# Loading the expert layers' weights in six later pieces, in a fused mLSTM and mixture-of-depths kernel

## The chip, the cores and the metric

The kernel runs on one core of one Trainium2 chip. The metric is the time on the device, in microseconds (us), of one launch; the median of three runs before the change is 186.09 us (185.08 to 186.35). A core has TensorE (PE in the profile, and PEld for its weight loads), VectorE (DVE), ScalarE (ACT), GpSimd (POOL), and SyncE (SP), which here only issues transfers (DMA).

## The reference: what is computed

The first half is an mLSTM cell over 4 batches, 8 heads, 768 positions and heads of 40 numbers; the second half sends the 128 best-scoring positions of each batch through two layers.

```python
# mLSTM, for every position t of (B=4, H=8, S=768, D=40)
m_new  = np.maximum(f_gate[:, :, t] + m, i_gate[:, :, t])
f_stab = np.exp(f_gate[:, :, t] + m - m_new)
i_stab = np.exp(i_gate[:, :, t] - m_new)
C = f_stab[..., None, None] * C + i_stab[..., None, None] * np.einsum('bhd,bhe->bhde', vt, kt)
n = f_stab[..., None] * n + i_stab[..., None] * kt
y[:, :, t] = sigmoid(o_gate) * (C @ qt) / np.maximum(np.abs(n @ qt), 1.0)
# bridge: y (B,H,S,D) -> x (B, S, 320)
# mixture of depths, for every batch b
scores  = x[b] @ w_gate
top_idx = the 128 positions with the highest scores
h  = np.maximum(x[b, top_idx] @ w1, 0.0)          # w1: 320 x 1024
ye = h @ w2                                       # w2: 1024 x 320
out[b] = x[b];  out[b, top_idx] += sigmoid(scores[top_idx])[:, None] * ye
```

## The kernel before

The positions are cut into chunks of 128, six to a batch, so there are 24 steps `n`, with batch `b = n // 6` and chunk `c = n % 6`. A prologue does steps 0 and 1; steps 2 to 23 run in a loop. Inputs are loaded ahead: step `n` issues the loads of step `n + 4` (`AHEAD = 4`, five buffers), and all of them, the stores of the results and the weights, go through the one queue of SyncE, in program order.

```python
def load_qk(n):                       # two transfers, 160 KB each
    for j, src in enumerate((k, q)):
        load_heads(n, qk_t[n % NB][:, j, :, 0:D], src)
...
def load_w1(j):                       # w1: 320 rows as three blocks of 128, 128 and 64
    d0, w = HW[j]
    for p in range(0, 128, w):        # the block of 64 rows is loaded twice, into both halves
        nc.sync.dma_start(out=w1[p:p + w, j, :], in_=moe_w1[d0:d0 + w, :])

def load_w2(j):
    f = slice(j * NFC // 2, (j + 1) * NFC // 2)
    nc.sync.dma_start(out=w2[:, f], in_=moe_w2.rearrange("(f p) d -> p f d", p=128)[:, f])
```

One step, cut to what is spoken of below. `within` writes pH (line 427), `exchange` pIC (396, 402), `products` pS (370), `turned` transposes k and q of step n + 2 into T (313, copied by ScalarE in 314), `weights` makes W = exp(...) (346, 347), masked by GpSimd (352), and `weighted` multiplies P = pS * W on VectorE (376).

```python
def step(n):
    load(n + AHEAD)
    pH = within(P[n], v1)
    ...
    give = exchange(*steps[n + 1], loaded[n + 1][0], T[n + 1], wv[n + 1])
    pS[n + 1] = products(T[n + 1])
    ...
    num, sor = norm(nums.get(n), pH, so)
    nums[n + 1] = exchanged(*steps[n + 1], *give)
    P[n + 1] = weighted(pS[n + 1], W[n + 1])
    ...
    W[n + 2] = weights(*steps[n + 2])
    layer(b, c)                       # a part of the layers of an earlier batch
    turned(n + 2)
    ...
    result(b, c, num, sor)            # x, and its store: out_dram<-x, line 448
    score(b, c, state[b][0])
    compare(...)                      # ge, line 470
```

`layer` spreads the two layers of one batch over six steps: with c = 3, 4 and 5 it computes columns 0 to 2, 3 to 5 and 6 to 7 of the first layer, with c = 0, 1 and 2 of the next batch the same groups of the second. The first use of the weights is therefore in steps 9, 10, 11 (w1) and 12, 13, 14 (w2).

```python
def first(self, f0, f1):              # ph, line 545
    for f in range(f0, f1):
        for j in range(NDC):
            nc.tensor.matmul(self.ph[:, f % 4, :], w1[:, j, f * 128:(f + 1) * 128], self.xeT[:, j, :], ...)
...
def second(self, f0, f1):             # py, line 569
    if f0 == 0:
        self.py = ps_m.tile([K_, DM], FP, name="py", tag="m")
    for f in range(f0, f1):
        nc.tensor.matmul(self.py, self.hT[:, f, :], w2[:, f, :], start=(f == 0), stop=(f == NFC - 1))
```

After step 3 the loop makes the constants with which positions are ranked; after steps 3 to 7 it loads the weights.

```python
for n in range(3, N):
    step(n)
    if n == 3:
        nc.gpsimd.iota(iota_i, pattern=[[1, K_]], channel_multiplier=0)
        nc.vector.tensor_copy(out=iota_f, in_=iota_i)            # line 847
        nc.gpsimd.iota(token_i, pattern=[[L, NT]], channel_multiplier=1)
        nc.vector.tensor_copy(out=token, in_=token_i)            # line 852
        nc.vector.tensor_scalar(out=later, in0=token_i, ...)     # line 854
        nc.gpsimd.memset(ones_b, 1.0)
        ...
    if 3 <= n < 3 + NDC:
        load_w1(n - 3)
    elif 3 + NDC <= n < 5 + NDC:
        load_w2(n - 3 - NDC)
```

The last batch's layers stand alone in the tail. Its first layer keeps all eight columns in eight PSUM banks at once; two banks are those of pS, the others are drawn from pools. The pool `ps_m` has two buffers, used in turn, and py is drawn from it afterwards.

```python
def first_at_once(self, banks):
    ph = [p[:, 0, 0:K_] for p in pS_t] + [pool.tile([128, K_], FP, name="ph", tag=tag) for pool, tag in banks]
    for f, p in enumerate(ph):
        for j in range(NDC - 1):
            nc.tensor.matmul(p, w1[:, j, f * 128:(f + 1) * 128], self.xeT[:, j, :], start=(j == 0), stop=False)
    for f, p in enumerate(ph):
        nc.tensor.matmul(p, w1[e, NDC - 1, ...], self.xeT[e, NDC - 1], start=False, stop=True)
    for f, p in enumerate(ph):        # odd columns on VectorE (line 561), even ones on ScalarE (line 563)
        ...
...
last.first_at_once([(ps_t, "t"), (ps_t, "t"), (ps_h, "h"), (ps_c, "c"), (ps_m, "m"), (ps_m, "m")])
last.gate()
last.gated()
last.second(0, NFC)
last.leave()
```

Of the kernel before, what the change touches and what calls it, by code (L numbers as in the profile page):

```python
# [8 lines left out]
FP = mybir.dt.float32  # L9
BF = mybir.dt.bfloat16  # L10
HF = mybir.dt.float16
I32 = mybir.dt.int32
U32 = mybir.dt.uint32
AF = mybir.ActivationFunctionType
OP = mybir.AluOpType
# [6 lines left out]
def kernel(  # L22
# [20 lines left out]
    nc = tc.nc  # L43

    B, H, S, D = q.shape
    L = 128
    NT = S // L
# [6 lines left out]
    NFC = F_ // 128  # L54
    HW = [(c, min(128, DM - c)) for c in range(0, DM, 128)]
    NDC = len(HW)
    K_ = capacity
# [9 lines left out]
    const = ctx.enter_context(tc.tile_pool(name="const", bufs=1))  # L67
# [5 lines left out]
    ps_t = ctx.enter_context(tc.tile_pool(name="ps_t", bufs=2, space=PSUM))  # L73
    ps_s = ctx.enter_context(tc.tile_pool(name="ps_s", bufs=1, space=PSUM))
    ps_c = ctx.enter_context(tc.tile_pool(name="ps_c", bufs=1, space=PSUM))
    ps_h = ctx.enter_context(tc.tile_pool(name="ps_h", bufs=1, space=PSUM))
    ps_m = ctx.enter_context(tc.tile_pool(name="ps_m", bufs=2, space=PSUM))
# [6 lines left out]
    def load_gates(eng, dst, src, g):  # L84
        for c in range(3):
# [20 lines left out]
                            channel_multiplier=-1)  # L106
# [52 lines left out]
    for j in range(2):  # L159
        nc.vector.tensor_reduce(out=of[:, j:j + 1], op=OP.add, axis=AX.XY,  # L160
                                in_=ident.rearrange("p (g x) -> p g x", x=32)[:, :, 12 * j:12 * j + 12])
# [16 lines left out]
    m = gate.tile([BH, NT + 1], FP, name="m")  # L178
# [5 lines left out]
    pS_t = [ps_s.tile([128, NP, L], FP, name=f"pS{j}") for j in range(2)]  # L184
# [34 lines left out]
    def level(g, pm):  # L219

        own = gate.tile([NR, 3], FP, name="own", bufs=2)
        nc.vector.tensor_tensor_reduce(out=own, in0=pm, in1=third, scale=1.0, scalar=0.0, op0=OP.mult, op1=OP.add,
                                       accum_out=m_in[g])
        nc.vector.tensor_scalar(out=FM[g][:, 1], in0=FM[g][:, 1], scalar1=m_in[g], scalar2=None, op0=OP.max)
        nc.vector.tensor_scalar(out=nM[g], in0=FM[g][:, 1, L - 1:L], scalar1=-1.0, scalar2=None, op0=OP.mult)

    def split(g, j, eng, rows=slice(0, NR)):
        x, xs = (FM[g][rows, 1], a[g][rows])[j], [part[rows] for part in parts[j][g]]
        rest = gate.tile([NR, L], FP, name=f"rest{j}", bufs=2)[rows]
        eng.tensor_copy(out=xs[0], in_=x)  # L230
        eng.tensor_tensor(out=rest, in0=x, in1=xs[0], op=OP.subtract)
        eng.tensor_copy(out=xs[1], in_=rest)
        eng.tensor_tensor(out=xs[2], in0=rest, in1=xs[1], op=OP.subtract)
# [58 lines left out]
    w1 = const.tile([128, NDC, F_], FP, name="w1")  # L292
# [3 lines left out]

        return out[0:b + 1].rearrange("b s d -> (b s) d")

    def load_w1(j):

        d0, w = HW[j]
        for p in range(0, 128, w):
            nc.sync.dma_start(out=w1[p:p + w, j, :], in_=moe_w1[d0:d0 + w, :])

    def load_w2(j):
        f = slice(j * NFC // 2, (j + 1) * NFC // 2)
        nc.sync.dma_start(out=w2[:, f], in_=moe_w2.rearrange("(f p) d -> p f d", p=128)[:, f])

    def turn(qk, j, T, copy=nc.scalar.copy):
# [11 lines left out]
    def gated(n):  # L321

        so = loaded[n][2]
        nc.scalar.activation(out=so, in_=so, func=AF.Tanh, scale=0.5)
        nc.scalar.add(so, so, 1.0)
# [29 lines left out]
    def scaled_v(b, c, v1):  # L355
        if c == NT - 1:
            return None
        wv = work.tile([128, H, D1], FP, name="wv")
        nc.gpsimd.tensor_tensor(out=wv, in0=v1[:, :, 0:D1], op=OP.mult,  # L359
                                in1=cols[c][:, 0, b * H:(b + 1) * H].unsqueeze(2).to_broadcast([128, H, D1]))  # L360
        return wv
# [11 lines left out]
    def weighted(pS, W):  # L373
        P = work.tile([128, NP, 2, L], FP, name="P", bufs=2)
        for j in range(2):
            nc.vector.tensor_tensor(out=P[:, :, j, :], in0=pS[j], op=OP.mult,  # L376
                                    in1=W.rearrange("p (n a) t -> p n a t", a=2)[:, :, j, :])
        return P
# [119 lines left out]
    def number(sel, token):  # L498

        pidx = ps_m.tile([K_, 1], FP, name="pidx", tag="m")  # L500
        for t in range(NT):
            nc.tensor.matmul(pidx, sel[:, t, :], token[:, t:t + 1], start=(t == 0), stop=(t == NT - 1))
        return pidx

    def gather(b, pidx):
        idx = mod.tile([K_, 1], U32, name="idx")
        nc.vector.tensor_scalar(out=idx, in0=pidx, scalar1=float(b * S), scalar2=None, op0=OP.add)
        xe = xe_t[b % 2]
        nc.gpsimd.indirect_dma_start(out=xe[0:K_, 0:DM], out_offset=None, in_=rows(b),
                                     in_offset=bass.IndirectOffsetOnAxis(ap=idx, axis=0),  # L510
                                     bounds_check=(b + 1) * S - 1, oob_is_err=False)
        return idx, xe

    class Layers:
# [34 lines left out]

        def first_at_once(self, banks):  # L550

            ph = [p[:, 0, 0:K_] for p in pS_t] + [pool.tile([128, K_], FP, name="ph", tag=tag) for pool, tag in banks]
            for f, p in enumerate(ph):
                for j in range(NDC - 1):
                    nc.tensor.matmul(p, w1[:, j, f * 128:(f + 1) * 128], self.xeT[:, j, :], start=(j == 0), stop=False)
            for f, p in enumerate(ph):
                e = HALVES[f % 2]
                nc.tensor.matmul(p, w1[e, NDC - 1, f * 128:(f + 1) * 128], self.xeT[e, NDC - 1], start=False, stop=True)
            for f, p in enumerate(ph):
                if f % 2:  # L560
                    nc.vector.tensor_scalar(out=self.hT[:, f, :], in0=p, scalar1=0.0, scalar2=None, op0=OP.max)
                else:
                    nc.scalar.activation(out=self.hT[:, f, :], in_=p, func=AF.Relu)  # L563
# [39 lines left out]
    def stated(n):  # L603
        wv[n] = scaled_v(*steps[n], loaded[n][1])
# [185 lines left out]
    turned(2)  # L790
    P[1] = weighted(pS[1], W[1])
    stated(1)
    level(1, pm)
    split(1, 0, nc.gpsimd)
    moving()
# [8 lines left out]
    scales(1)  # L804
    gated(1)
    nc.vector.tensor_scalar(out=of_which, in0=which, scalar1=of[:, 1:2], scalar2=None, op0=OP.mult)
    P[2] = weighted(pS[2], W[2])

    load(1 + AHEAD)
# [3 lines left out]
    for j in range(2):  # L813
# [15 lines left out]
                            pattern=[[-1, L]], channel_multiplier=1)  # L829
# [11 lines left out]
    for n in range(3, N):  # L841
        step(n)
        if n == 3:
            iota_i = const.tile([128, K_], I32, name="iota_i")
            nc.gpsimd.iota(iota_i, pattern=[[1, K_]], channel_multiplier=0)
            iota_f = const.tile([128, K_], FP, name="iota_f")
            nc.vector.tensor_copy(out=iota_f, in_=iota_i)

            token_i = const.tile([128, NT], I32, name="token_i")
            nc.gpsimd.iota(token_i, pattern=[[L, NT]], channel_multiplier=1)  # L850
            token = const.tile([128, NT], HF, name="token")
            nc.vector.tensor_copy(out=token, in_=token_i)
            later = const.tile([128, NT], FP, name="later")
            nc.vector.tensor_scalar(out=later, in0=token_i, scalar1=-1.0, scalar2=float(S - 1), op0=OP.mult, op1=OP.add)
            ones_b = const.tile([128, 1], BF, name="ones_b")
            nc.gpsimd.memset(ones_b, 1.0)
            xe_t = [const.tile([128, NDC * 128], FP, name=f"xe{n}") for n in range(2)]
            for xe in xe_t:
                nc.gpsimd.memset(xe[:, DM:], 0.0)
        if 3 <= n < 3 + NDC:  # L860
            load_w1(n - 3)
        elif 3 + NDC <= n < 5 + NDC:
            load_w2(n - 3 - NDC)


    b, u = steps[-1]
# [2 lines left out]
    n = u * L  # L869
# [12 lines left out]
                                   op0=OP.is_ge, op1=OP.mult, accum_out=cnt[:, u:u + 1])  # L882
    pend = ps_h.tile([128, NT], FP, name="pend", tag="h")
    for t in range(NT):
# [3 lines left out]
                                   op0=OP.add, op1=OP.add)  # L888
# [3 lines left out]
    last = Layers(b, None, None)  # L892
# [6 lines left out]
    for j, (d0, w) in enumerate(HW):  # L899
# [3 lines left out]
        if j < 2:  # L903
# [4 lines left out]
    nc.scalar.copy(out=last.xeT[HALVES[1], 2], in_=pX[3][HALVES[1]])  # L908
    nc.vector.tensor_copy(out=last.xeT[HALVES[0], 2], in_=pX[2][HALVES[0]])
    last.idx, last.xe = gather(b, number(sel_h, token))  # L910
    last.first_at_once([(ps_t, "t"), (ps_t, "t"), (ps_h, "h"), (ps_c, "c"), (ps_m, "m"),
                        (ps_m, "m")])
    last.gate()
    last.gated()
    last.second(0, NFC)
# [27 lines left out]
```

## Time and profile before

| | |
|---|---|
| time, median of 3 (range) | 186.09 us (185.08 to 186.35) |
| span of the profiled execution, mean granted TensorE clock | 183.5 us, 0.986 |
| busy: PE, PEld | 170.4 us (93%), 141.5 us (77%) |
| busy: DVE, ACT, POOL | 135.9 us (74%), 102.3 us (56%), 106.4 us (58%) |
| transfers | 105,938 packets, 24.70 MB, mean 135 GB/s |
| share of the transfers' engines taken by SyncE's queue | 78.7% |
| chain that ended last | PE 64%, issue 10%, DVE 8%, DMA 7%, ACT 4% |
| one input's load: KB, issue to landing | 160.0 KB, 4.6 to 5.1 us (medians by input) |
| the weights' transfers, KB | w1: 2 x 512.0 and 2 x 256.0; w2: 2 x 640.0 |

The profile is one execution. Its page cuts the span into 40 equal slices of 4.6 us and gives a digit, in tenths, for each engine's busy share, the granted clock of TensorE and the transfers. A busy TensorE is not a TensorE at its peak: matmuls are pipelined, and their ends are modelled. The chain that ended last is followed back from the last instruction, at each step to what released it. In a timeline a line has its start, its busy time, the engine, the line of the kernel, the operation, what is written and read, and a count; a bracket gives the idle time before it and what ended that. SPq is SyncE's queue of issues; the time beside an issue is that of issuing it, not of moving the data.

### The profile page before, as it was taken

The page shows a single profiled execution, that of the slowest core. Times are in us where ns is not written, and L with a number is a line of the kernel's source. Part 1 is how long each engine was busy: PE and PEld are TensorE (multiplying, and loading weights), DVE is VectorE, ACT ScalarE, POOL GpSimd, SP SyncE. Part 2 cuts the span into 40 slices and gives each one's busy share as a digit, 9 for nine tenths or more (in the row PEclk, how much of TensorE's full clock was granted, in tenths as well). Part 3 has the DMA queues.
Part 4 walks back from the last instruction along what each step waited for, and adds up shares of the span by engine and source line. Part 5 has one row for each costly group of instructions (what it writes and reads, how often), then busy time and mean ns, then how long its engine had stood idle before and what let it go on. Part 6 is the DMA issues. An engine that isn't in the chain of part 4 may idle for free.

```text
span 183.5 us, 7319 instructions
## 1 busy us (share of the span) xinstructions
PE 170.4 (93%) x2992; PEld 141.5 (77%) x2992; DVE 135.9 (74%) x403; ACT 102.3 (56%) x250; POOL 106.4 (58%) x176
## 2 busy tenths in 40 slices
PE   7889997998999699999999999999999999989990
PEld 2578886787787587898797888898878979869860
DVE  7857788898789837568998969788988788584210
ACT  3285779899998687375545465465635652201100
POOL 7987986778887865137859633546666361113202
PEclk9999999999999969999999999999999999999998
DMA  3999998999998999999899999979972101010100
GB/s 73 148 149 136 159 163 156 156 173 231 156 205 178 151 266 147 222 157 183 160 177 165 192 170 190 163 145 178 176 80 75 39 36 41 36 39 36 38 4 36
DMA packets 105938, 24.70 MB, mean 135 GB/s; under 512 B 100656, under 2 KB 105264, under 8 KB 105904
## 3 DMA queue, kind: packets, MB, share of 16 engines
q1 hardware_dynamic: 105088, 22.77, 78.7%
q0 software_dynamic: 384, 1.31, 2.4%
q8 instruction: 24, 0.39, 1.0%
q10 hardware_dynamic: 432, 0.15, 0.6%
q14 instruction: 10, 0.08, 0.2%
HBM read 19.63 MB, written 4.59 MB: 132 GB/s over the span
## 4 chain that ended last, share of the span: by engine, by line
PE 64%; issue 10%; DVE 8%; DMA 7%; ACT 4%; SPq 2%; POOL 2%; POOLq 1%; DVEq 0%
PE pH L427 12%; PE pS L370 11%; PE pt L313 10%; PE ph L545 10%; PE py L569 5%; PE pIC L396 5%; PE pIC L402 4%; PE pW L346 3%; DMA qk<-in_q_dram 3%; DMA out_dram<-ye,idx 2%; DMA xe<-out_dram,idx 2%; PE pO L247 1%; DVE P L376 1%; DVE ge L470 1%; ACT T L314 1%
## 5 line engine op out<-in xcount | busy, mean ns | idle before, releaser
L347 ACT ACTIVATE W<-pW 128x512 f32<-128x512 f32 x48 | 26.1, 598 | 22.1 <-PE pW L346 21.9
L442 POOL TENSOR_TENSOR sor<-so,rec 128x320 f32<-128x320 f32 x24 | 17.8, 741 | 32.4 <-DVE rec L440 32.1
L376 DVE TENSOR_TENSOR P<-pS,W 128x512 f32<-128x512 f32 x48 | 30.9, 686 | 4.6 <-POOL W L352 2.4
L314 ACT COPY T<-pt 128x512 f32<-128x512 f32 x47 | 25.4, 589 | 14.1 <-PE pt L313 14.0
L352 POOL TENSOR_SCALAR_AFFINE_SELECT W<-W 128x512 f32<-128x512 f32 x46 | 30.6, 688 | 3.6 <-ACT W L347 3.6
L427 PEld LDWEIGHTS pH<-v,P 128*64 128x64 f32 x768 | 25.2, 141 | 8.8 <-DVE x L447 3.2
L427 PE MATMUL pH<-v,P 128*64 128x64 f32 x768 | 28.5, 229 | 2.7 <-issue 1.3
L313 PE MATMUL pt<-ident,qk 128*128 128x128 f32 x192 | 25.8, 276 | 1.8 <-DMA qk<-in_k_dram 1.0
L470 DVE SCALAR_TENSOR_TENSOR ge<-sb,sc,earlier 128x128 bf16<-128x128 f32 (+5 forms) x23 | 17.4, 761 | 13.0 <-ACT sb L464 13.0
L370 PE MATMUL pS<-T 64*64 64x64 f32 (+1 forms) x768 | 26.2, 255 | 0.0
L313 PEld LDWEIGHTS pt<-ident,qk 128*128 128x128 f32 x192 | 21.1, 141 | 4.1 <-ACT scr L455 1.4
L370 PEld LDWEIGHTS pS<-T 64*64 64x64 f32 x768 | 20.4, 132 | 1.9 <-issue 0.7
L569 PE MATMUL py<-w,hT 128*128 128x320 f32 x64 | 19.4, 444 | 0.4 <-ACT hT L563 0.4
L359 POOL TENSOR_TENSOR wv<-v,cols 128x328 f32<-128x328 f32 x20 | 14.9, 743 | 7.2 <-DMA v<-in_v_dram 5.2
L545 PE MATMUL ph<-xeT,w 128*128 128x128 f32 x144 | 18.1, 280 | 0.0
L545 PEld LDWEIGHTS ph<-xeT,w 128*128 128x128 f32 x144 | 16.7, 192 | 1.5 <-issue 1.5
L575 POOL DMA_INDIRECT out_dram<-ye,idx x4 | 4.6, 1140 | 19.6 <-DVE ye L573 19.6
L569 PEld LDWEIGHTS py<-w,hT 128*128 128x128 f32 x64 | 11.5, 191 | 5.6 <-issue 1.4
L396 PE MATMUL pIC<-C,T 128*64 128x82 f32 x320 | 15.8, 241 | 0.0
L396 PEld LDWEIGHTS pIC<-C,T 128*64 128x64 f32 x320 | 13.2, 141 | 0.3 <-issue 0.2
L384 POOL TENSOR_TENSOR C<-C,cols 128x328 f32<-128x328 f32 x16 | 13.1, 819 | 0.1
L432 DVE TENSOR_TENSOR pH<-num,pH 128x328 f32<-128x328 f32 x20 | 10.0, 499 | 3.7 <-PE pH L427 3.6
(166 smaller groups left out, 284.1 us busy)
## 6 DMA issues: line engine op xcount, KB each, us to landing
qk<-in_k_dram SPq DMA_DIRECT2D x24, 160.0 KB, 4.7
qk<-in_q_dram SPq DMA_DIRECT2D x24, 160.0 KB, 4.7
v<-in_v_dram SPq DMA_DIRECT2D x24, 160.0 KB, 5.1
so<-in_o_gate_dram SPq DMA_DIRECT2D x24, 160.0 KB, 4.6
out_dram<-x SPq DMA_DIRECT2D x24, 160.0 KB, 4.0
w<-in_moe_w_dram SPq DMA_DIRECT2D x2, 640.0 KB, 4.7
w<-in_moe_w_dram SPq DMA_DIRECT2D x2, 512.0 KB, 4.5
w<-in_moe_w_dram SPq DMA_DIRECT2D x2, 256.0 KB, 4.5
```

What stands on the lines that cost most here:

```text
L313: nc.tensor.transpose(pt[:, p, :], qk[:, j, 2 * p:2 * p + 2, :].rearrange("s a d -> s (a d)"), ident)
L314: copy(out=T[:, j], in_=pt)
L347: nc.scalar.activation(out=W[:, h0:h0 + 4, :], in_=pW, func=AF.Exp)
L352: nc.gpsimd.affine_select(out=W[:, h0:h0 + 4, :], in_=W[:, h0:h0 + 4, :], compare_op=OP.is_ge, fill=0.0, base=0, pattern=[[0, 4], [1, L]], ...
L370: nc.tensor.matmul(pS_t[j][s, p, ts], T[e, 0, p, s], T[e, 1, p, ts], start=True, stop=True)
L376: nc.vector.tensor_tensor(out=P[:, :, j, :], in0=pS[j], op=OP.mult, in1=W.rearrange("p (n a) t -> p n a t", a=2)[:, :, j, :])
L396: nc.tensor.matmul(pI[t, 2 * p * D1:2 * (p + 1) * D1], T[:, 1, p, t], C[:, p].rearrange("e a d -> e (a d)"), start=True, stop=True)
L427: nc.tensor.matmul(pH[t, 2 * p + j, :], P[:, p, j, t], v1[:, 2 * p + j, :], start=True, stop=True)
L442: nc.gpsimd.tensor_tensor(out=sor, in0=so, in1=rec.unsqueeze(2).to_broadcast([128, H, D]), op=OP.mult)
L470: nc.vector.scalar_tensor_tensor(out=ge[:, GE[u]:GE[u + 1]], in0=sb.rearrange("p t l -> p (t l)")[:, 0:n], scalar=sc[:, u:u + 1], in1=earl ...
L545: nc.tensor.matmul(self.ph[:, f % 4, :], w1[:, j, f * 128:(f + 1) * 128], self.xeT[:, j, :], start=(j == 0), stop=(j == NDC - 1))
L569: nc.tensor.matmul(self.py, self.hT[:, f, :], w2[:, f, :], start=(f == 0), stop=(f == NFC - 1))
```

## The change

Three things change; what is computed does not.

- The weights were loaded by blocks of rows (w1) and in halves (w2) after steps 3 to 7, long ahead of use. Now each is cut into three pieces by the columns of the first layer (3, 3 and 2 of 8), which are the groups that `layer` uses, and a piece is loaded after steps 7, 8, 9 (w1) and 10, 11, 12 (w2), two steps ahead of its first use. This is to keep the weights from standing in the queue ahead of inputs that are needed sooner.
- The constants of the ranking are made in the prologue, not after step 3. The zeroing of the `xe` pads stays.
- In the tail's first layer the eight columns take the banks in another order: the drawn ones first, in the order h, c, m, m, t, t, and those of pS last.

```diff
-    def load_w1(j):
-
-        d0, w = HW[j]
+    def load_w1(f):
+
+        f = slice(f.start * 128, f.stop * 128)
+        d0, w = HW[-1]
+        nc.sync.dma_start(out=w1[:, 0:NDC - 1, f], in_=moe_w1[0:d0, f].rearrange("(j p) f -> p j f", p=128))
         for p in range(0, 128, w):
-            nc.sync.dma_start(out=w1[p:p + w, j, :], in_=moe_w1[d0:d0 + w, :])
-
-    def load_w2(j):
-        f = slice(j * NFC // 2, (j + 1) * NFC // 2)
+            nc.sync.dma_start(out=w1[p:p + w, NDC - 1, f], in_=moe_w1[d0:d0 + w, f])
+
+    def load_w2(f):
         nc.sync.dma_start(out=w2[:, f], in_=moe_w2.rearrange("(f p) d -> p f d", p=128)[:, f])
...
-            ph = [p[:, 0, 0:K_] for p in pS_t] + [pool.tile([128, K_], FP, name="ph", tag=tag) for pool, tag in banks]
+            ph = [pool.tile([128, K_], FP, name="ph", tag=tag) for pool, tag in banks] + [p[:, 0, 0:K_] for p in pS_t]
...
     stated(1)
+    iota_i = const.tile([128, K_], I32, name="iota_i")
+    nc.gpsimd.iota(iota_i, pattern=[[1, K_]], channel_multiplier=0)
+    ...
+    nc.gpsimd.iota(token_i, pattern=[[L, NT]], channel_multiplier=1)
+    ...
+    nc.gpsimd.memset(ones_b, 1.0)
     level(1, pm)
...
     nc.vector.tensor_scalar(out=of_which, in0=which, scalar1=of[:, 1:2], scalar2=None, op0=OP.mult)
+    nc.vector.tensor_copy(out=iota_f, in_=iota_i)
+    nc.vector.tensor_copy(out=token, in_=token_i)
+    nc.vector.tensor_scalar(out=later, in0=token_i, scalar1=-1.0, scalar2=float(S - 1), op0=OP.mult, op1=OP.add)
     P[2] = weighted(pS[2], W[2])
...
         if n == 3:
-            ... (the iotas, copies, later and ones_b, as above)
             xe_t = [const.tile([128, NDC * 128], FP, name=f"xe{n}") for n in range(2)]
...
-        if 3 <= n < 3 + NDC:
-            load_w1(n - 3)
-        elif 3 + NDC <= n < 5 + NDC:
-            load_w2(n - 3 - NDC)
+        if 0 <= n - NT - 1 < 6:
+            piece = n - NT - 1
+            f0 = 3 * (piece % 3)
+            (load_w1, load_w2)[piece // 3](slice(f0, min(f0 + 3, NFC)))
...
-    last.first_at_once([(ps_t, "t"), (ps_t, "t"), (ps_h, "h"), (ps_c, "c"), (ps_m, "m"),
-                        (ps_m, "m")])
+    last.first_at_once([(ps_h, "h"), (ps_c, "c"), (ps_m, "m"), (ps_m, "m"), (ps_t, "t"), (ps_t, "t")])
```

More of the change, by code (lines that the diff above doesn't have):

```diff
@@ L792 @@
     stated(1)
+    iota_i = const.tile([128, K_], I32, name="iota_i")
+    nc.gpsimd.iota(iota_i, pattern=[[1, K_]], channel_multiplier=0)
+    iota_f = const.tile([128, K_], FP, name="iota_f")
+    token_i = const.tile([128, NT], I32, name="token_i")
+    nc.gpsimd.iota(token_i, pattern=[[L, NT]], channel_multiplier=1)
+    token = const.tile([128, NT], HF, name="token")
+    later = const.tile([128, NT], FP, name="later")
+    ones_b = const.tile([128, 1], BF, name="ones_b")
+    nc.gpsimd.memset(ones_b, 1.0)
     level(1, pm)
@@ L843 @@
         if n == 3:
[L844 to L856, printed above, removed]
             xe_t = [const.tile([128, NDC * 128], FP, name=f"xe{n}") for n in range(2)]
```

## The prediction, made before the changed kernel ran

> **What bounds the kernel now.** I read the page's forty slices first, then the queue that issues the transfers (the timeline of SyncE), then the chain that ended last, then the timelines of TensorE, ScalarE and VectorE where that chain leaves TensorE. From the page, granted clock, transfers, rate:
>
> ```profile
> PEclk9999999999999969999999999999999999999998
> DMA  3999998999998999999899999979972101010100
> GB/s 73 148 149 136 159 163 156 156 173 231 156 205 178 151 266 147 222 157 183 160 177 165 192 170 190 163 145 178 176 80 75 39 36 41 36 39 36 38 4 36
> ```
>
> The DMA engines are full from the second slice to about the thirtieth (4.6 us a slice, so to 137 us). The slices at 205 to 266 GB/s fall where the weights move; the others carry inputs in short packets at about 155. One slice, the fifteenth (64.2 to 68.8 us), has a clock of 0.6.
>
> The queue of issues shows what the weights cost. Number the k loads by step: the one at 36.19 is load 7, at 57.61 load 10, at 78.56 load 13, at 103.63 load 18. Columns: start, issue time, what.
>
> ```profile
> 36.19 0.39 SPq L121 DMA_DIRECT2D qk<-in_k_dram  x1
> ...
> 42.01 0.42 SPq L303 DMA_DIRECT2D w<-in_moe_w_dram  x1
> ...
> 48.64 0.42 SPq L303 DMA_DIRECT2D w<-in_moe_w_dram  x1
> ...
> 55.45 2.13 SPq L303 DMA_DIRECT2D w<-in_moe_w_dram  x2
> 57.61 0.59 SPq L121 DMA_DIRECT2D qk<-in_k_dram  x1
> ...
> 64.35 0.43 SPq L307 DMA_DIRECT2D w<-in_moe_w_dram  x1
> ...
> 72.08 0.43 SPq L307 DMA_DIRECT2D w<-in_moe_w_dram  x1
> ...
> 78.56 1.80 SPq L121 DMA_DIRECT2D qk<-in_k_dram  x1
> ...
> 103.63 0.38 SPq L121 DMA_DIRECT2D qk<-in_k_dram  x1
> ```
>
> Without weights a step's four loads and one store take (103.63 - 78.56) / 5 = 5.0 us of queue. From load 7 to load 13, six steps, it took 42.4; so 42.4 - 30.1 = 12.3 us went to the weights, 2816 KB by the page's issue table: 4.4 us per 1000 KB.
>
> The chain that ended last is TensorE almost without a break from 65 us to 157 us. Before that it leaves TensorE twice: at 28 to 42 us (VectorE, GpSimd), and at 58 to 64 us for a transfer, which TensorE's timeline shows (bracket: idle before, and releaser):
>
> ```profile
> 62.99 0.63 PE L313 MATMUL pt<-ident,qk 128*128 128x128 f32 x4 [1.01 <-DMA qk<-in_k_dram]
> 64.20 0.63 PE L313 MATMUL pt<-ident,qk 128*128 128x128 f32 x4 [0.58 <-DMA qk<-in_q_dram]
> ...
> 65.80 1.98 PE L427 MATMUL pH<-v,P 128*64 128x64 f32 x32
> 67.56 1.31 PE L396 MATMUL pIC<-C,T 128*64 128x82 f32 x16
> ```
>
> In step 8 TensorE waits for load 10, then runs step 9 slowly: 1.98 us for the pH group (1.15 in other steps), 1.31 for pIC (0.74), 0.86 for its second half (0.61). So the first half is governed by the queue, the second by TensorE.
>
> **What the Trainium skill says.** "TensorE: Matmul & The Clock Gate", Part 1, says that an idle activity window lets the clock drop to half for a window. The trace agrees in kind: the windows view gives a mean clock of 0.80 at 66 to 74 us, right after the wait. "DMA: Bandwidth & Descriptors", Queues, rings and completion order, says that an engine takes the descriptors of one ring in order; so weights issued ahead of a load delay it, as the 12.3 us show. The same page, Why small descriptors are slow, gives packets a fixed cost; here 100,656 of 105,938 packets are under 512 B and the mean is 135 GB/s. "SBUF — State Buffer" tells of a port pair for which VectorE and GpSimd exclude each other; the cast of only 128x6 numbers below took 0.61 us beside a GpSimd select, which fits, though it proves nothing.
>
> **The change, part by part.**
>
> (a) Constants. They sit on VectorE between the comparisons of step 3 and the sum of step 4:
>
> ```profile
> 38.19 0.64 DVE L847 CAST iota_f<-iota_i 128x128 f32<-128x128 int32 x1
> 38.76 0.61 DVE L852 CAST token<-token_i 128x6 f16<-128x6 int32 x1
> 39.28 0.16 DVE L854 TENSOR_SCALAR later<-token_i 128x6 f32<-128x6 int32 x1
> 39.35 0.49 DVE L432 TENSOR_TENSOR pH<-num,pH 128x328 f32<-128x328 f32 x1
> ```
>
> From 38.19 to 39.35 is 1.2 us, and the chain runs through it. But ScalarE works without a gap from 34.5 us to its copy of T at 45.74, where it had waited only 0.21 us. So of the 1.2 us I let 0.3 through. In the prologue VectorE waits 1.17 us for a masked W before P[2] (at 19.96): the three operations fit there. GpSimd's two iotas and the memset (0.24, 0.14, 0.11 us) meet 0.36 us of idle time ahead of that mask. Cost 0 to 0.2 us, and TensorE does not wait there; I take 0.
>
> (b) Weights leave the way of loads 8 to 11. Load 10 had three w1 transfers (1536 KB, 1536 x 4.4 / 1000 = 6.7 us) ahead of it; now none. The wait of 1.01 + 0.58 = 1.6 us goes. So should the half clock after it: 0.83 + 0.57 + 0.25 = 1.65 us. With (a), step 9 starts its layer 0.3 + 1.6 + 1.65 = 3.5 us sooner.
>
> (c) Weights become a deadline. The pieces are 576, 576, 384, 480, 480 and 320 KB: 2.5, 2.5, 1.7, 2.1, 2.1 and 1.4 us of queue. The bytes are the same. With load 7 as before at 36.2, loads 8 to 11 go out every 5.0 us, and the first piece, behind the store of step 7, at 36.2 + 5 x 5.0 = 61.2. Each next piece comes 5.0 us plus the previous piece later. Landing: 4.6 us after issue (median of this tile's transfers), and 1.0 more for w1, whose piece is three issues of about 0.5 us. "Wanted" is the start of the layer's matmuls in TensorE's timeline of before, less 3.5 us:
>
> - step 9: issue 61.2, lands 66.8; was 72.57, wanted 69.1
> - step 10: 68.7, lands 74.3; was 77.78, wanted 74.3
> - step 11: 76.2, lands 81.8; was 83.92, wanted 80.4: waits 1.4, the gain falls to 2.1
> - step 12: 82.9, lands 87.5; was 90.13, now wanted 88.0
> - step 13: 90.0, lands 94.6; was 96.76, now wanted 94.7
> - step 14: 97.1, lands 101.7; was 103.19, now wanted 101.1: waits 0.6, the gain falls to 1.5
>
> So about 2 us of the 3.5 are given back: by step 14 the queue has moved the same bytes as before, and the kernel can be ahead only by what the last piece arrives ahead of its use. Afterwards TensorE is the bound and carries 1.5 us to the end.
>
> (d) The bank order of the tail. Every matmul stays; only which bank holds which result changes. The sum py takes the bank of the first ph drawn from the same pool. That was column 6, evicted last on ScalarE; it becomes column 2, evicted second.
>
> ```profile
> 173.35 0.71 ACT L563 ACTIVATE hT<-ph 128x128 f32<-128x128 f32 x3
> ...
> 174.11 4.07 PEld L569 LDWEIGHTS py<-w,hT 128*128 128x128 f32 x16 [0.55 <-ACT hT L563]
> 174.11 4.57 PE L569 MATMUL py<-w,hT 128*128 128x320 f32 x16 [0.36 <-ACT hT L563]
> ```
>
> TensorE idles 0.36 us until the third of the group of evictions is out, at 174.06. Now it can begin when the last ph ends. Column 6 is then needed only six matmul pairs later. I count the whole 0.35 us, since ye waits for py.
>
> Sum: 1.5 + 0.35 = 1.85 us; 186.1 - 1.9 = 184.2 us.
>
> **Rivals.** First: the pieces arrive in time, since my cost per byte holds w1's last third, loaded as two transfers of 64 rows and taking longest (load 10 came 8.5 us after load 9). If the new pieces run 2 us cheaper in all, nothing waits and 3.5 + 0.35 remain: 182.2. Second: the pieces of w1 are rows of 1536 and 1024 B instead of 4096 B. If that costs 2 us more, the last piece lands 2 us later and the gain is gone: about 186. Third: waits of 1 to 2 us ahead of a layer let the clock drop again. One drop costs about 1.65 us, part of which hides in the next wait: about 185.5. For it speaks that 1.6 us was enough once; against it, that these waits come singly with TensorE busy around them. Fourth: ScalarE already set the pace in steps 4 to 8, and w1 in the queue hurt only one step; then (b) is as counted.
>
> **Range and chances.** The landing times carry some 2 us of error in either direction, and that moves the time almost one for one, from 182.2 (no waits, cap) to 186; a clock drop adds up to 0.6. So 182.0 to 186.6. Faster by over 2% means below 182.4, where nearly no piece may wait: 0.17. Slower by over 2% needs above 189.8: two clock drops and late pieces: 0.03. Within 2%: 0.80.
>
> **What the profile would show.** Right: no wait of L313 for a transfer in step 8, no slice with a clock of 0.6 near 64 us; the pH group of step 9 at 1.15 us near 64.0; waits of the ph or py matmuls for w, 0.5 to 2 us each, in steps 11 to 14; the constants at 18.6 to 20 us with P[2] at most 0.3 later; py in the tail starting with no wait for ScalarE. Wrong: w landing early with no such waits (then faster); or a first piece after 70 us, or a new dip of the clock (then slower).

## The result, and the profile after

The changed kernel ran in 183.41 us (median of 4 executions, 183.22 to 184.28; a fifth took 186.33 us, at a mean granted clock of 0.987), the kernel before in 186.09 us (185.08 to 186.35): a ratio of 0.9875, with a 95% interval of 0.9827 to 0.9923. The prediction was 184.2 us, in a range of 182.0 to 186.6. One thing is needed to read every number below: the kernel before scatters. In the first set of experiments it ran 59 times, from 182.6 to 187.3 us, with a median of 184.85; in 20 of them the mean granted clock of TensorE was 0.991 or less, and those had a median of 186.0 us, the others 184.55. The profile before, at 0.986, is of the same kind. Each experiment is therefore compared with the runs of before made beside it. The ratios leave out executions more than 1.5% above the fastest of the same kernel in their set (that fifth too), while the medians of the sets hold all.

From the page of the changed kernel, the granted clock, the share of the transfers and their rate in 40 slices:

```profile
PEclk9999999999999999999999999999999999999999
DMA  3999999999998999999999999889962101010100
GB/s 72 153 148 138 155 158 179 180 171 177 166 160 164 229 179 224 194 160 236 143 208 208 193 175 176 154 167 173 160 68 76 40 36 40 36 40 36 38 0 36
```

The slice with a clock of 0.6 is gone. The transfers are as full as before, from the second slice to about the thirtieth; only the stretch with high rates has moved, from 41 us and later to 59 us and later. The queue's timeline tells the same (loads 7 and 11, three of the six pieces, load 18):

```profile
35.76 0.39 SPq L121 DMA_DIRECT2D qk<-in_k_dram  x1
...
55.38 1.22 SPq L121 DMA_DIRECT2D qk<-in_k_dram  x1
...
59.98 0.42 SPq L303 DMA_DIRECT2D w<-in_moe_w_dram  x1
...
88.78 0.43 SPq L308 DMA_DIRECT2D w<-in_moe_w_dram  x1
...
95.85 0.43 SPq L308 DMA_DIRECT2D w<-in_moe_w_dram  x1
...
101.81 0.39 SPq L121 DMA_DIRECT2D qk<-in_k_dram  x1
```

Without weights a step takes (55.38 - 35.76) / 4 = 4.9 us; from load 11 to load 18 the queue needed 46.4 us for seven steps, so 46.4 - 34.3 = 12.1 us went to the weights, against 12.3 before (11.3 with the 5.0 us a step of before). The work of the queue is about the same, in another order. Load 18 goes out at 101.81 where it was 103.63.

TensorE's timeline, at step 9 and at steps 13 and 14:

```profile
64.13 1.15 PE L428 MATMUL pH<-v,P 128*64 128x64 f32 x32 [0.34 <-DVE x L448]
...
94.00 1.88 PE L570 MATMUL py<-w,hT 128*128 128x320 f32 x6 [0.52 <-DMA w<-in_moe_w_dram]
...
102.54 0.52 PE L526 MATMUL pX<-ident,xe 128*128 128x128 f32 x3 [0.77 <-DMA xe<-out_dram,idx]
...
103.97 1.15 PE L428 MATMUL pH<-v,P 128*64 128x64 f32 x32
```

No line of the transposes pt waits for a transfer any more, and step 9 runs its pH in 1.15 us. Two waits are new: 0.52 us for the second piece of w2 in step 13, and 0.77 us in step 14 for `xe`, the gather of batch 1's chosen rows. The start of pH gives the lead of the changed kernel over the one before, step by step:

| step | pH before, us | after, us | lead, us |
|---|---|---|---|
| 2 | 27.07 | 27.09 | -0.02 |
| 5 | 42.49 | 41.88 | 0.61 |
| 8 | 58.40 | 58.09 | 0.31 |
| 9 | 65.80 | 64.13 | 1.67 |
| 10 | 74.78 | 71.52 | 3.26 |
| 13 | 93.32 | 89.97 | 3.35 |
| 14 | 99.75 | 96.99 | 2.76 |
| 15 | 105.78 | 103.97 | 1.81 |
| 23 | 157.19 | 155.38 | 1.81 |

In the tail the last sum py starts at 171.88 instead of 174.11, a lead of 2.23; the spans are 181.3 and 183.5 us. The timeline of the tail has the eviction of three columns from ScalarE, then py, then the eviction of the fourth:

```profile
171.37 0.66 ACT L564 ACTIVATE hT<-ph 128x128 f32<-128x128 f32 x3 [4.09 <-PE ph L559]
...
171.88 4.57 PE L570 MATMUL py<-w,hT 128*128 128x320 f32 x16
171.98 0.28 ACT L564 ACTIVATE hT<-pS 128x128 f32<-128x128 f32 x1
```

py no longer has a bracket: it begins while ScalarE is still evicting.

### The profile page after: what moved, and what is told of

It reads as the page before. It is cut to its first block, busy times and chain, and to the rows that moved or that the text cites. A ratio compares the mean times of both kernels' runs of the same rounds, so it can differ in the third digit from the quotient of the medians.

```text
span 181.3 us, 7327 instructions
## 1 busy us (share of the span) xinstructions
PE 169.9 (94%) x2992; PEld 140.1 (77%) x2992; DVE 135.8 (75%) x403; ACT 102.1 (56%) x250; POOL 105.8 (58%) x176
## 4 chain that ended last, share of the span: by engine, by line
PE 61%; issue 12%; ACT 10%; DMA 7%; POOL 5%; DVE 3%; POOLq 1%
PE pH L428 10%; PE ph L546 10%; PE pS L371 10%; PE pt L314 8%; PE pIC L397 5%; DMA xe<-out_dram,idx 5%; PE pIC L403 4%; PE pW L347 3%; PE py L570 3%; PE pS L190 3%; ACT W L348 2%; ACT M_o L258 2%; POOL W L353 2%; ACT T L315 2%; DMA out_dram<-ye,idx 2%
## 5 line engine op out<-in xcount | busy, mean ns | idle before, releaser
L315 ACT COPY T<-pt 128x512 f32<-128x512 f32 x47 | 25.3, 589 | 12.8 <-PE pt L314 12.3
L428 PEld LDWEIGHTS pH<-v,P 128*64 128x64 f32 x768 | 24.4, 138 | 8.6 <-DVE x L448 3.5
L428 PE MATMUL pH<-v,P 128*64 128x64 f32 x768 | 27.6, 225 | 2.5 <-issue 1.3
L471 DVE SCALAR_TENSOR_TENSOR ge<-sb,sc,earlier 128x128 bf16<-128x128 f32 (+5 forms) x23 | 18.1, 792 | 13.0 <-ACT sb L465 12.9
L397 PE MATMUL pIC<-C,T 128*64 128x82 f32 x320 | 15.2, 236 | 0.0
L397 PEld LDWEIGHTS pIC<-C,T 128*64 128x64 f32 x320 | 12.7, 137 | 0.3 <-issue 0.2
L448 DVE TENSOR_TENSOR x<-pH,sor 128x320 f32<-128x320 f32 x24 | 11.6, 485 | 1.1 <-POOL sor L443 1.1
```

Of the source, the lines that this page charges most:

```text
L315: copy(out=T[:, j], in_=pt)
L397: nc.tensor.matmul(pI[t, 2 * p * D1:2 * (p + 1) * D1], T[:, 1, p, t], C[:, p].rearrange("e a d -> e (a d)"), start=True, stop=True)
L428: nc.tensor.matmul(pH[t, 2 * p + j, :], P[:, p, j, t], v1[:, 2 * p + j, :], start=True, stop=True)
L471: nc.vector.scalar_tensor_tensor(out=ge[:, GE[u]:GE[u + 1]], in0=sb.rearrange("p t l -> p (t l)")[:, 0:n], scalar=sc[:, u:u + 1], in1=earl ...
```

## The experiments

The theory is that of the prediction: the queue moves a fixed amount, the place of the weights in it decides which use waits, and the wait lets the clock drop. The rivals are that the constants' 1.2 us on VectorE are the gain, that cutting the weights is, or that the half clock is chance. Medians are set beside those of the kernel before in the same set.

| run | median, us | before, us | ratio (95% interval) |
|---|---|---|---|
| e1_weights | 184.21 | 184.85 | 0.9956 (0.9927 to 0.9984) |
| e2_constants | 185.08 | 184.85 | 1.0037 (1.0003 to 1.0071) |
| e3_banks | 184.49 | 184.85 | 1.0005 (0.9976 to 1.0033) |
| e4_from6 | 182.15 | 184.85 | 0.9868 (0.9815 to 0.9922) |
| after_again | 183.93 | 184.65 | 0.9929 (0.9901 to 0.9957) |
| e5_filler | 184.50 | 184.65 | 0.9999 (0.9976 to 1.0023) |
| e8_blocks | 183.72 | 184.65 | 0.9928 (0.9902 to 0.9953) |
| e9_from5 | 182.73 | 184.65 | 0.9904 (0.9871 to 0.9937) |
| e10_enter_later | 183.01 | 184.68 | 0.9916 (0.9890 to 0.9943) |
| e7_double_w2 | 186.49 | 184.68 | 1.0148 (1.0091 to 1.0206) |
| e6_from3 | 185.84 | 184.68 | 1.0106 (1.0054 to 1.0159) |
| e11_enter_next | 182.29 | 184.64 | 0.9851 (0.9807 to 0.9896) |

### The three parts one by one

**e1_weights**: the kernel before with the new `load_w1`, `load_w2` and the loop over pieces.

> The kernel before with the six later pieces of the weights alone (constants after step 3, old bank order). Queue theory: the wait for load 10 in step 8 and the half clock after it go, step 9's layer starts about 3.0 us sooner, and waits in steps 13 and 14 (for a piece of w2 and for the gather) bring the lead to the same 1.8 us that the full change has: 186.1 - 1.8 = 184.3 us. Rival, in which the constants' 1.2 us on VectorE count in full: this run lacks them and stands at about 185.0 us or above.

184.21 us, the level expected and below the rival's; but before stood at 184.85 in this set, so the gain is 0.6 us by the medians, 0.4% by the ratio. The weights alone give part of the gain, in two ways. Only 1 of the 22 executions has a clock of 0.991 or less, against 20 of 59 of before; and the medians of the executions above 0.991 are 184.18 and 184.55. The waits came in other steps than expected: 0.40 us in step 11, for the last piece of w1, and 1.01 us in step 12, for the first of w2:

```profile
81.46 0.71 PE L546 MATMUL ph<-xeT,w 128*128 128x128 f32 x4 [0.40 <-DMA w<-in_moe_w_dram]
...
89.14 1.85 PE L570 MATMUL py<-w,hT 128*128 128x320 f32 x6 [1.01 <-DMA w<-in_moe_w_dram]
```

**e2_constants**: the kernel before with the iotas moved ahead of `level(1, pm)` and the copies ahead of `P[2]`.

> The kernel before with the constants made in the prologue alone. Queue theory: steps 5 to 8 start 0.3 us sooner, but load 10 lands where it did, so TensorE waits that much longer in step 8 and the clock drops all the same: 186.1 us, at most 0.3 less. Rival: the 1.2 us that leave VectorE's path are a gain of 1 us or more: 185.0 us.

No gain by the ratio. 10 of the 22 executions fell to 0.991 or less; the other 12 have a median of 184.31, 0.24 us under those of before, within the 0.3 expected and not to be told from nothing. TensorE's timeline shows where the earlier start went:

```profile
62.68 0.63 PE L313 MATMUL pt<-ident,qk 128*128 128x128 f32 x4 [0.38 <-DMA qk<-in_q_dram]
...
69.03 0.63 PE L313 MATMUL pt<-ident,qk 128*128 128x128 f32 x4 [0.76 <-DMA qk<-in_k_dram]
71.09 0.63 PE L313 MATMUL pt<-ident,qk 128*128 128x128 f32 x4 [1.43 <-DMA qk<-in_q_dram]
```

Step 8 begins at 58.14 instead of 58.40, and TensorE then waits 0.38 us for load 10 and 0.76 + 1.43 us for load 11, which in the profile of before was hidden by the slow step 9. Beside the profile of e3_banks, at full clock too and with the constants in their old place, the lead is 0.37 us at step 8 (58.14 against 58.51), 0.15 at step 10 and 0.07 at step 15. So what a step gains ahead of this place is mostly returned at the queue.

**e3_banks**: the kernel before with the new order of banks.

```diff
-            ph = [p[:, 0, 0:K_] for p in pS_t] + [pool.tile([128, K_], FP, name="ph", tag=tag) for pool, tag in banks]
+            ph = [pool.tile([128, K_], FP, name="ph", tag=tag) for pool, tag in banks] + [p[:, 0, 0:K_] for p in pS_t]
...
-    last.first_at_once([(ps_t, "t"), (ps_t, "t"), (ps_h, "h"), (ps_c, "c"), (ps_m, "m"), (ps_m, "m")])
+    last.first_at_once([(ps_h, "h"), (ps_c, "c"), (ps_m, "m"), (ps_m, "m"), (ps_t, "t"), (ps_t, "t")])
```

> The kernel before with the new bank order of the tail alone. If py's wait for the bank of column 6 was the whole of it: 0.4 us less, 185.7 us, and no idle time of TensorE before py for ScalarE. Rival: what py really waits for is the eviction of column 0, which is no sooner: no change.

The times cannot resolve it: an interval of -0.24% to +0.33% holds both 0 and 0.4 us. The trace can. From the start of pidx, the matmuls just ahead of the tail's first layer, to the start of py, e3_banks takes 172.87 - 167.86 = 5.01 us, e2_constants, with the old order, 173.22 - 167.79 = 5.43, as the kernel before (174.11 - 168.68). So 0.42 us, and the last output waits for py in all of them.

### Is the half clock the wait's doing?

**after_again**: the changed kernel, in a set with others.

> The changed kernel as it is, on the same chip as the runs beside it. The kernel before ran from 182.6 to 187.3 us in the last set (median 184.85), and its slower executions are those with a mean clock of 0.991 or less: a half clock somewhere. Queue theory: the change takes away the wait that lets the clock drop, so its executions lie closer together, none at 0.991 or less, median 183.4 us as before, 1.4 us ahead of a median of 184.85. Rival, in which the half clock is chance and not the wait: it shows in a third of the executions here too.

183.93 us, and 2 of 18 executions at a clock of 0.991 or less, against 10 of 47 of before in this set (in the first set 20 of 59; the 22 in e5_filler's expectation is a miscount). Without those executions the medians are 183.63 and 184.54. So the change does not quite end the half clock. That it becomes rarer these 18 executions do not show by themselves; e1_weights does, with 1 of 22 against 20 of 59. The ratio of this set, with more executions, puts the gain nearer 0.7% than the first comparison's 1.25%.

**e5_filler**: the kernel before, with work of no use in the place of the waits.

```diff
+            if n == NT + 2:
+                T[n + 2] = work.tile([128, 2, NP, L], FP, name="T")
+                for j in range(2):
+                    filler(5 if j == 0 else 3)      # 128x512 matmuls into a bank nobody reads
+                    turn(loaded[n + 2][0], j, T[n + 2])
... (in step 9 likewise, 3 and 3)
```

> The kernel before, with matmuls of no use put ahead of the transposes of steps 8 and 9 (5 and 3 in step 8, 3 and 3 in step 9, of about 0.2 us each, written to a bank nobody reads), so that TensorE works where it had waited for loads 10 and 11. The transfers stay as they were. If the idle time makes the clock drop, executions at 0.991 or less become rare (they were 22 of 59), and the slow end of the spread, 186 us and above, goes; the median stays at the queue's pace, 184.5 us or up to 0.5 above, as the loads land no sooner. Rival, in which the drop has another cause: a third of the executions still have it.

None of 14 executions fell to 0.991, and they lie between 184.16 and 184.87 us, where before ranged from 183.47 to 188.67. The median is 184.50, that of the undropped executions of before (184.54). This makes the rival unlikely: at a rate of 10 in 47, 14 executions without a drop would have a chance of about 1 in 28. Busy in that stretch, TensorE kept its clock, with the transfers in the same order. It also parts the two gains: the drop cost 1.5 to 1.7 us (186.0 or 186.2 against 184.5) where it came, and without it the time stays where the queue puts it.

### Place or cutting?

**e6_from3**: the changed kernel with its pieces after steps 3 to 8 (`piece = n - 3`).

> The changed kernel with its pieces after steps 3 to 8: cut as in the change, but about where the weights stood before. If only the place in the queue counts, load 10 again has three pieces (1536 KB) ahead of it, TensorE waits in steps 8 or 9 by 1 to 2 us in all, some executions fall to a mean clock of 0.991 or less, and the time is that of the kernel before less the tail's 0.4: 184.2 us. If the cutting itself helps, as the clock drops no more or the pieces move faster: 183 us or less.

185.84 us, above both branches, and three of four executions at 0.991 or less. Its TensorE timeline is that of before again, with the wait, and a clock of 0.50 from 66 to 69 us:

```profile
64.32 0.63 PE L314 MATMUL pt<-ident,qk 128*128 128x128 f32 x4 [1.74 <-DMA qk<-in_q_dram]
...
66.09 1.98 PE L428 MATMUL pH<-v,P 128*64 128x64 f32 x32
```

Pieces in the old place bring nothing, and the constants and banks do not save it. Why it is above the kernel before (the one execution at full clock took 185.67 us) stays open; four executions are few.

**e8_blocks**: the weights uncut (blocks of w1 after steps 5, 6, 7, halves of w2 after 8 and 9), constants and banks as in the change.

> Constants and banks as in the change, but the weights uncut, as blocks and halves, and only moved: w1 after steps 5, 6, 7, w2 after steps 8 and 9. If the place in the queue is all that counts, load 10 has one block ahead of it (2.2 us) and still lands in time, load 11 two; the last block of w1 lands near 70 us, about 0.7 us after step 9 wants it (69.3), and w2 is in well before its use: no waits in steps 13 and 14 for w2, 182.5 us. If cutting is what makes the change work, all three blocks are needed at once in step 9, TensorE waits there by 2 us or more, and the time is 184 us or above.

183.72 us: short of the 182.5 expected for pure place, under the 184 expected for pure cutting, and equal to the changed kernel (0.9928 and 0.9929); 3 of the 22 executions are at 0.991 or less. No use of w2 waits; but step 9 does, for the last block of w1:

```profile
71.82 1.83 PE L545 MATMUL ph<-xeT,w 128*128 128x128 f32 x14 [1.70 <-DMA w<-in_moe_w_dram]
```

So cutting is not needed for the gain. What it buys is that step 9 needs a third of w1, not all of it; what this run waits there, 1.70 us, the changed kernel waits in steps 12 to 14, 1.3 us in all.

### The new waits

**e4_from6**: every piece one step sooner (`piece = n - 6`).

> The changed kernel with every piece loaded one step sooner (after steps 6 to 11, three steps ahead of use). If the waits in steps 13 and 14 (0.5 us for w2, 0.8 us for the gather) are both due to the weights' bytes in the queue, both go, and the lead of 3.3 us of step 12 lasts: 183.4 - 1.5 = 181.9 us. If the gather is slow by itself, only the first wait goes: about 182.8 us. If loads 11 and 12, now behind a piece more, come late, a wait returns in steps 9 or 10 and the time is 183.4 us or more.

182.15 us, between the first and the second branch. The wait for w2 is gone, that for the gather is smaller and stays:

```profile
101.74 0.52 PE L526 MATMUL pX<-ident,xe 128*128 128x128 f32 x3 [0.47 <-DMA xe<-out_dram,idx]
```

**e9_from5**: two steps sooner (`piece = n - 5`).

> The changed kernel with every piece two steps sooner (after steps 5 to 10, four steps ahead of use). Queue theory: load 10 has one piece ahead of it (2.5 us), load 11 two (5.0 us); they land near 58.6 and 66.2 us, wanted at 61.6 and 68.3, so still no wait; no piece is waited for; the gather of batch 1 meets inputs alone in the queue. 181.8 us, a little under the 182.15 of the pieces from step 6. If the slack of load 11 is less than that, a wait returns in step 9: 183 us.

182.73 us, expected 181.8. Loads 10 and 11 still come in time, and no piece is waited for, as foretold; but pX in step 14 still waits 0.78 us for the gather. The last piece goes out at 87.83, some ten microseconds ahead of it, and the gather itself is quick, 4.04 us; but it is issued only at 97.86, where the changed kernel issued it at 96.48. Its indices were ready at 95.69, but GpSimd had this operation and the masks of W (1.53 us from 96.18) ahead of it:

```profile
95.48 0.74 POOL L360 TENSOR_TENSOR wv<-v,cols 128x328 f32<-128x328 f32 x1 [1.62 <-DMA v<-in_v_dram]
```

wv waited for the v of load 15. So with the weights two steps sooner an input came late in their stead, and the wait only changed hands.

**e10_enter_later**: e4_from6 with pX behind the step's own transposes, in steps 14 and 20.

```diff
-            elif c == 2:
-                enter(b - 1)
             if n + 2 < N and n > NT + 3:
                 turned(n + 2)
+            if c == 2:
+                enter(b - 1)
```

> The pieces from step 6, and in steps 14 and 20 the transposes of the step's k and q put ahead of those of the gathered rows (pX), so that the gather of batch 1 has 1.0 us more. With the pieces from steps 6 and 5, pX of step 14 waited 0.47 and 0.78 us for that gather. If that wait is on the path, it goes: about 0.5 us under the pieces from step 6, 181.6 us. If the k and q transposes or ScalarE's copies take its place, no change: 182.1 us.

A miss: 183.01 us. pX does not wait, but the transpose behind it does, for the bank that pX's copy still holds:

```profile
103.50 0.32 PE L464 MATMUL pb<-ident,sc 128*128 128x128 f32 x1 [0.78 <-ACT xeT L528]
```

Steps 14 and 20 take 7.02 us each, where those of e4_from6 take 6.69 and 6.02. Nor does this profile show that the later place ended the wait for the gather: that had landed at 99.73, 3.50 us after its issue, before pX would have started in either order.

**e11_enter_next**: e4_from6 with pX after pH of the next step.

```diff
         pH = within(P[n], v1)
+        if b > 1 and c == 3:
+            layers[b - 1].enter()
...
             elif c == 2:
-                enter(b - 1)
+                layers[b - 1] = Layers(b - 1, *picked[b - 1])
```

> The pieces from step 6, and the gathered rows of batches 1 and 2 transposed one step later, right after pH of steps 15 and 21 (their first use, ph, follows some 3 us after). Putting them only behind the k and q transposes had turned TensorE's wait for the gather into a wait of pb for ScalarE's copy, which holds the bank that pb needs (0.78 us, in both steps). Here pb no longer stands behind that copy, and the gather has about 2 us more. If both waits were on the path: about 0.5 us under the 182.15 us of the pieces from step 6, 181.6 us. If the copy now delays ph in steps 15 and 21: 182.2 us or more.

182.29 us. Neither wait is left, and steps 14 and 15 together take 13.28 us instead of 13.77; yet the whole is not to be told from e4_from6. The time is that of the second branch, but not by its cause: the copy ends at 105.24, ph starts at 107.29. This execution was 0.17 us behind e4_from6 at step 7 already and lost 0.54 us more in steps 8, 9 and 13. Both versions beat the kernel before by 1.3 to 1.5% and lie below the changed kernel's two medians, though not in one set with it.

### What does a byte in the queue cost?

**e7_double_w2**: the changed kernel, with each piece of w2 loaded twice.

```diff
+    spare = const.tile([128, 3, DM], FP, name="spare")
     def load_w2(f):
+        nc.sync.dma_start(out=spare[:, 0:f.stop - f.start], in_=moe_w2.rearrange("(f p) d -> p f d", p=128)[:, f])
         nc.sync.dma_start(out=w2[:, f], in_=moe_w2.rearrange("(f p) d -> p f d", p=128)[:, f])
```

> The changed kernel with each piece of w2 loaded twice, the first time into a tile that nobody reads: 1280 KB more in the queue. If it is bytes in the queue that make pieces late, at 4.4 us per 1000 KB the pieces of w2 land 2.1, 4.2 and 5.6 us later than in the changed kernel, py waits in steps 12 to 14 for about that in sum, and the time is 5 us above it: 188.5 to 189.5 us. Rival, in which the queue has room and the waits are only latency from issue to landing: 1 us or less above it, 184.5 to 185.

```profile
89.97 1.85 PE L573 MATMUL py<-w,hT 128*128 128x320 f32 x6 [2.79 <-DMA w<-in_moe_w_dram]
...
97.97 1.88 PE L573 MATMUL py<-w,hT 128*128 128x320 f32 x6 [1.32 <-DMA w<-in_moe_w_dram]
```

186.49 us, 2.6 to 3.1 above the changed kernel's two medians: neither the 5 us of the theory nor the 1 us of the rival. In step 13, behind 960 KB more, py starts 3.0 to 4.0 us later than in the two profiles of the changed kernel (94.98 and 94.00), so 3.1 to 4.1 us per 1000 KB; the first piece, behind 480 KB more, landed 1.8 to 3.6 us later (89.84 against 88.02 and 86.23). The bytes do make pieces late, by about the 2.1 and 4.2 us foretold. The sum of the waits was wrong: they are 2.79 + 1.32 = 4.1 us, 2.8 more than in the changed kernel, close to the loss measured. The third piece is not waited for, since its use has moved back as far as its issue (py of step 14 from 100.43 to 104.55, the issue from 95.85 to 100.30): a delay that TensorE has taken once it does not take again.

## Why the prediction was right

- **The bound** was read rightly: the queue in the first half, TensorE afterwards. e2_constants shows it best, as a gain ahead of the queue is returned by it.
- **(a) Constants.** 0.3 us was let through; the lead is 0.31 us at step 8, and the prologue lost 0.02. Alone, this part shows no gain that can be told from nothing.
- **(b) Loads 10 and 11 freed.** Foretold 3.5 us of lead (0.3 + 1.6 + 1.65), measured 3.26 at step 10 (0.31 + 1.36 + 1.59). Ahead of load 10 stood four transfers of w1, not three; their sum of 1536 KB is right. But I took one profile's half clock for the kernel's habit. It is in a fifth to a third of its executions, so that 1.65 us is not a term of every run. And where the clock does not drop, another wait stands in its place (in e2_constants that for load 11): e3_banks, with the old weights at full clock, starts step 10 at 73.91, only 0.87 us ahead of the 74.78 of before. In the set of after_again the whole change gained 0.7 us by the medians, where 1.85 was foretold. That the time came so near is partly luck: the base of 186.1 us was 1.2 to 1.5 us above the medians of the later sets, and the gain was foretold about 1.1 us too large.
- **(c) Weights as a deadline.** The giving back was foretold at 2.0 us and measured as 1.5; the place was wrong. I had waits in steps 11 and 14 for weights. There was 0.59 us of lead lost in step 13, 0.52 of it the wait for w2, and 0.95 in step 14, of which 0.77 was the wait for the gather, which the prediction did not name. The mis-sized term is the issue: the pieces went out up to 1.6 us sooner than in my table (59.98, 68.45, 74.60, 81.81, 88.78 and 95.85 against 61.2, 68.7, 76.2, 82.9, 90.0 and 97.1). The table starts 1.2 us late; from the first piece to the last the table has 35.9 us and the run 35.87, so the cost per byte held. The last piece of w1, 1.6 us sooner, had landed at 80.10 when ph of step 11 started at 80.57, so nothing was given back there; in e1_weights it went out at 76.85 and was waited for. In the second profile of the changed kernel the gather is not waited for: pX starts 5.1 us after its issue, as in the kernel before, where it did not wait either. There the waits are 1.17 us at step 12, which ended as the first piece of w2 landed (though the profile names ScalarE's `W`), and 0.15 us at step 13. So the place of the wait differs from one execution to the next, and its sum hardly: 1.29 and 1.32 us in these two profiles, 1.41 in e1_weights.
- **(d) The tail.** Foretold 0.35 us, measured 0.42, from the order of the banks and nothing else.
- **The rivals.** The first (pieces in time, 182.2 us) is what e4_from6 comes near by issuing sooner, not by cheaper pieces: 182.15. The second, short rows dearer, did not come: 12.1 us of queue against 12.3. The third, a new half clock, is in 2 of 18 executions and in the fifth of the first comparison; where in the kernel it falls is not known, as none of the three was profiled. The fourth fits in its outcome: up to step 8 the weights alone bring no lead (e1_weights starts it at 58.52, the kernel before at 58.40).

## What to carry to other kernels

When a queue works without a break, moving a transfer later does not remove its cost but hands it to another user; look for the order in which each load lands just ahead of its use, and give the large, early-known ones one step of slack more than seems needed. Before pricing an idle gap, see how many executions have its aftermath: a profile is one execution. And look at how much room the other transfers have before a user moves forward: the gather here had about 5 us between issue and use before and after the change, and took 3.5 to 5.9, so that it is waited for in one execution and not in the next.

## What the runs showed of the hardware

Two profiles show a half clock. In that of the kernel before, TensorE waited 1.01 and 0.58 us with work between, ending at 64.2 us, and the granted clock was 0.50 from 66 to 69 us; in e6_from3 the waits were 0.26 and 1.74 us, ending at 64.3, and the clock was 0.50 in the same stretch. In e2_constants waits of 0.38, 0.76 and 1.43 us, spread from 62 to 71 us, left it at 1.00, and so did single waits of 1.70 us (e8_blocks) and 2.79 us (e7_double_w2). So the length of a wait does not tell by itself whether the clock drops. A mean clock of 0.991 or less was seen in 20 of 59 executions of the kernel before, which took about 1.5 us longer than the others; with matmuls of no use in the gap all 14 executions stayed above 0.991, at no cost in the median.

The gather of batch 1's 128 rows, on GpSimd's own queue, took from 3.50 us (e10_enter_later) to 5.92 us (the changed kernel) from issue to landing, beside the full queue of loads; at the end of the kernel before, where that was empty, a gather took 2.98.
